# The state's part of a linear-attention output, computed per head in quarters of the array, with a compact state

## Chip, cores and metric

One core of a Trainium2 chip runs the whole kernel in one launch. The metric is the device time of an execution in microseconds; lower is better. All inputs and the output are fp32 in device memory.

## What is computed

For 4 batches, 8 heads, 768 steps and a head size of 48, a linear attention with a decaying state per head, and on its output (3072 tokens of 384 values) a layer with three input matrices, a maximum and an output matrix:

```python
for t in range(768):
    cur = einsum('bhd,bhe->bhde', u * k[t], v[t])
    y[t] = einsum('bhd,bhde->bhe', r[t], state + cur)
    state = w[t][..., None] * state + einsum('bhd,bhe->bhde', k[t], v[t])
x = y.transpose(0, 2, 1, 3).reshape(3072, 384)
h = maximum(maximum(x @ w1, x @ w2), x @ w3)      # 384 -> 768
out = h @ w_out                                   # 768 -> 384
```

## The kernel before

**Tiling.** The recurrence is done in chunks of 128 steps (`C`), 6 per batch and 24 in all, numbered k (`NK`). The 8 heads stand as 4 pairs (`NP`): the first head of a pair in partitions 0 to 47, the second in 64 to 111. The layer works on 512 tokens at a time, a "half" in the program's words, so there are six of them, each fed by 4 chunks (`CPH`). The first half's layer uses plain fp32 matmuls; the other five split every operand into a high and a low part and use three matmuls for one.

**The steps of a chunk** have one letter each (line 459). `b`, `f`, `r` (L309 to L335): running products of the decay by two scans on VectorE, then r and k are scaled by them; `b` also copies the chunk's total decay into `dec` on ScalarE, one copy for each head of the pairs (L315). `c` (L339) is a range check on ScalarE. `d`, `e` (L341 to L370): the diagonal term and the empty score tile. `X` scores (L374): per pair two matmuls of 48 partitions, one from partition 0 and one from 64, into two PSUM banks. `M` take (L386): VectorE copies the scores under the causal mask. `T` transposes (L395). `R` from_state (L404): what the state of all earlier chunks gives to the output, one matmul per pair, with the two heads' states as diagonal blocks of one 112 x 128 operand `sstar`, so the array sums over both heads' partitions and the zero blocks keep the heads apart. `U` to_state (L412): the chunk's contribution to the state, 8 matmuls into one bank; in chunks 1 to 3 it also adds the old state by two matmuls with the identity, one for each block column (L422). `S` state (L426): VectorE adds the old state (from chunk 4 on, one add for each head of the pairs, L433) and multiplies by the next chunk's decay, into both block columns at once (L435). `V` values (L439): scores times v, 8 matmuls that add to R's result in the tile `y`. `E` result (L447): ScalarE copies `y` to the layer's input `x`; after four chunks, six small DMAs put the fourth pair's rows where the layer wants them. `n` loads.

R and the first step of V write the same tile: `y` comes from a pool of one bank (`ps_y`), but chunks 1 and 3 take a bank of the layer's pool instead (`spare`, L406), and so do their scores (L377). PSUM's eight banks go: two for scores, one for `y`, one for T and U, four for the layer (`ps_m`, L187 to L190). The layer's pool also serves the small matmuls of `e` in the first 8 chunks (L356) and warm-up matmuls (`W`, L472).

**Order.** All engines work in program order. The strings at L67 to L70 write the order of the steps out by hand: a letter, then how many chunks ahead; `|` ends a unit. FRONT is used for chunks 0 to 2, LAST for 3, TURN and ORD for 4, ORD for the rest. In FRONT, R of the next chunk is issued at the end of a chunk (`R1`), before that chunk's M and V; in ORD, R of a chunk stands first, followed by X of the next chunk, U and V. A second string (START, L73) mixes units (`a`), weight conversions (`c`, `f`) and layer groups (`m`); later one group of the layer follows another and units are put in evenly (L604).

**The layer** (`moe_groups`, L111). A group is one bank: 6 plain or 9 split matmuls of 512 columns (L144). Its reader is issued after the next group's matmuls: ScalarE's copy (L123) for the first of three matrices, VectorE's maximum (L126) for the others. The output stage (L164) has four tiles of 384 columns, copied out by ScalarE (L168).

A second program part (from L611) repeats everything in another way where the range check fails; it does not run here.

Of the kernel before, what the change touches and what calls it, by code (L numbers as in the profile page):

```python
# [42 lines left out]
NP = 4  # L43
# [23 lines left out]
FRONT = "w U0 b1 | d1 f1 r1 | w e1 c1 S0 W2 X1 T1 | R1 M0 | V0 E0 n3 |"  # L67
LAST = "w M0 | V0 E0 U0 W9 n3 | b1 d1 | f1 r1 w | e1 c1 S0 X1 T1 R1 |"
# [19 lines left out]
def kernel(ctx: ExitStack, tc, tin, nat, u_flat, u_pair, v_t, w_all, out, ytr):  # L88
# [84 lines left out]
    with ExitStack() as fast:  # L173
# [16 lines left out]
        ps_m = pool("ps_m", 4, space=PSUM)  # L190
# [42 lines left out]
        sstar = [cst.tile([128, NP, 2, 64], F32, name=f"sstar{i}") for i in range(2)]  # L233
        dec = [cst.tile([128, LINE], F32, name=f"dec{i}")[:, 0:2 * NP].rearrange("p (a b) -> p a b", a=NP) for i in range(2)]
        for t in dec:
            nc.gpsimd.memset(t[:, :, :], 0.0)
        for t in sstar:
            nc.gpsimd.memset(t[:, :, :, :], 0.0)
# [70 lines left out]
        def prep_scan_b(k):  # L309
            gf = g_p.tile([128, lines(2 * WC)], F32, name="gf")[:, 0:2 * WC].rearrange("p (a b) -> p a b", a=2)  # L310
            t = tbuf[k % NB]
            nc.vector.tensor_tensor_scan(out=gf[0:112, 0, ::-1], data0=t[0:112, 0:WC][:, ::-1],  # L312
                                         data1=d_bwd[0:112, ::-1], initial=0.0, op0=ALU.mult, op1=ALU.add)
            for hh, rows in enumerate((slice(0, 64), slice(64, 112))):
                nc.scalar.copy(out=dec[k % 2][rows, :, hh], in_=gf[rows, 0, 1:WC:WS])  # L315
            prep[k] = dict(gf=gf)
# [86 lines left out]

        def from_state(k):  # L404
            p = prep[k]
            spare = k < CPH and k % 2  # L406
            p["y"] = y = ps_m.tile([128, NP, C], F32, name="psm") if spare else ps_y.tile([128, NP, C], F32, name="y")
            for pr in range(NP if k % NCH > 0 else 0):
                nc.tensor.matmul(y[:, pr, :], lhsT=sstar[k % 2][0:112, pr, :, :].rearrange("p a b -> p (a b)"),  # L409
                                 rhs=p["rp"][0:112, pr, :], start=(pr == 0), stop=True, skip_group_check=True)  # L410

        def to_state(k):  # L412
            if goes_on(k):
                p = prep[k]
                p["pu"] = pu = ps_tu.tile([128, 512], F32, name="tu")
                for pr in range(NP):
                    for q, m in ((0, 64), (64, 48)):
                        h = 2 * pr + (q > 0)
                        nc.tensor.matmul(pu[q:q + m, pr * D:(pr + 1) * D],  # L419
                                         lhsT=p["kn"][:, pr, q:q + m], rhs=natt[k][0][:, h * D:(h + 1) * D],  # L420
                                         start=(pr == 0), stop=(pr == NP - 1), skip_group_check=True)
                for hh in range(2 if k % NCH > 0 and k < CPH else 0):  # L422
                    nc.tensor.matmul(pu[0:112, 0:NP * D], lhsT=ident[0:112, 0:112], rhs=sstar[k % 2][0:112, :, hh, 0:D],
                                     start=False, stop=True, skip_group_check=True)

        def state(k):  # L426

            if goes_on(k):
                new = prep[k]["pu"][0:112, 0:NP * D].rearrange("p (a b) -> p a b", a=NP)
                if k % NCH > 0 and k >= CPH:  # L430
                    cur = scur[0:112, :].rearrange("p (a b) -> p a b", a=NP)
                    for hh, rows in enumerate((slice(0, 64), slice(64, 112))):
                        nc.vector.tensor_tensor(out=cur[rows], in0=new[rows], in1=sstar[k % 2][rows, :, hh, 0:D], op=ALU.add)  # L433
                    new = cur
                nc.vector.tensor_tensor(out=sstar[(k + 1) % 2][0:112, :, :, 0:D],  # L435
                                        in0=new.unsqueeze(2).broadcast_to([112, NP, 2, D]),
                                        in1=dec[(k + 1) % 2][0:112, :, :].unsqueeze(3).broadcast_to([112, NP, 2, D]), op=ALU.mult)

        def values(k):  # L439
            p = prep[k]  # L440
            for pr in range(NP):
                for q, m in ((0, 64), (64, 48)):
                    h = 2 * pr + (q > 0)
                    nc.tensor.matmul(p["y"][q:q + m, pr, :], lhsT=natt[k][0][:, h * D:h * D + m], rhs=p["a"][:, h, :],  # L444
                                     start=(k % NCH == 0 and pr == 0), stop=True, skip_group_check=True)

        def result(k):  # L447
# [5 lines left out]
            nc.scalar.copy(out=x[0:112, :, slot * C:(slot + 1) * C], in_=prep[k]["y"][0:112, :, :])  # L453
# [24 lines left out]
        def attn():  # L478
            for step in "bdfeWrRXTcW":
# [132 lines left out]
    with tc.If(rv != 0), ExitStack() as slow:  # L612
# [9 lines left out]
        with tc.For_i(0, B) as b:  # L622
            for pr in range(NP):
# [16 lines left out]
                for j in range(KT):  # L640
                    with tc.For_i(0, 16) as i:
# [21 lines left out]
                        for hh in range(2):  # L663
                            if pr < KT:
                                dst = ytr[pr, ds(i + 64 * hh + 16 * j, 1), ds(b, 1), :]
                            else:
                                dst = ytr[j, ds(i + 64 * hh + 48, 1), ds(b, 1), :]
# [41 lines left out]

def _layout(r, k, v, w, u, moe_w1, moe_w2, moe_w3, moe_w_out):  # L710
# [19 lines left out]
    for j in range(KT):  # L730
        for half in range(2):
            row[j, 64 * half:64 * half + 48] = (2 * j + half) * D + np.arange(48)
            row[j, 64 * half + 48:64 * half + 64] = (6 + half) * D + 16 * j + np.arange(16)
# [27 lines left out]
```

## Time and profile before

| | us |
|---|---|
| median of 3 runs | 435.39 |
| lowest and highest | 434.93, 436.48 |
| span of the profiled execution (its only time on the page) | 434.7 |
| TensorE busy in it | 422.1 |
| VectorE busy | 288.5 |
| ScalarE busy | 155.8 |
| GpSimd busy | 63.3 |

The span goes from the first to the last instruction of the profiled execution. PE is the matrix engine TensorE, PEld its weight loads, DVE VectorE, ACT ScalarE, POOL GpSimd, SP SyncE, which issues most DMAs. A group of the profile is all instructions of one line, engine and shape. The chain is followed back from the last instruction, at each step to what released it. Matmuls are pipelined and a group's mean duration is longer than the distance between two of them, so rates are read from the chain or from starts, not from the means.

### The profile page before, as it was taken

The numbers are of one execution on the slowest core, as the hardware profiler recorded it, in microseconds if no ns is written. First come the engines' busy times: TensorE is split into PE (matmuls) and PEld (weight loads), VectorE is DVE, ScalarE is ACT, GpSimd is POOL, SyncE is SP. The second block draws the span as 40 slices with busy tenths as digits, with TensorE's granted clock in tenths as the row PEclk, the third lists the DMA queues.
The fourth block names the chain that finished last, engine by engine and source line by source line (L and its number), as shares of the span: only waits on it lengthen the run. The fifth ranks groups of instructions, "written<-read, shape, count | busy, mean of one in ns | idle before, by whom it ended". The sixth has DMA issues, their size and how long they took to land.

```text
span 434.7 us, 7072 instructions
## 1 busy us (share of the span) xinstructions
PE 422.1 (97%) x2767; PEld 337.7 (78%) x2767; DVE 288.5 (66%) x520; ACT 155.8 (36%) x342; POOL 63.3 (15%) x69
## 2 busy tenths in 40 slices
PE   7997999999999999999999999999999999999994
PEld 3784645546788888988889988889988889988893
DVE  5999999999769987837658638648548624223310
ACT  1447554554453444423213423222523221312211
POOL 3120110020333030312112112202112100000000
PEclk9999999999999999999999999999999999999998
DMA  8883944344181403280411270340370000200001
GB/s 215 247 265 88 368 113 164 90 146 111 38 242 51 118 10 110 49 280 1 120 54 65 55 250 26 120 114 5 89 240 2 0 2 1 90 3 2 0 22 60
DMA packets 17244, 43.76 MB, mean 101 GB/s; under 512 B 2432, under 2 KB 8704, under 8 KB 17200
## 3 DMA queue, kind: packets, MB, share of 16 engines
q1 hardware_dynamic: 16832, 42.61, 32.1%
q10 hardware_dynamic: 368, 0.59, 0.5%
q8 instruction: 24, 0.39, 0.4%
q14 instruction: 20, 0.16, 0.1%
HBM read 37.30 MB, written 4.72 MB: 97 GB/s over the span
## 4 chain that ended last, share of the span: by engine, by line
PE 94%; DVE 2%; ACT 1%; DMA 1%; issue 0%; POOL 0%; DVEq 0%; POOLq 0%; ACTq 0%
PE psm L144 54%; PE psm L164 17%; PE gram L383 6%; PE y L444 5%; PE y L409 4%; PE tu L419 2%; PE psm L475 2%; PE tu L400 2%; PE psm L358 1%; DMA x<-x 1%; ACT cv L287 0%; ACT cv L271 0%; DVE x_lo L104 0%; DVE a L390 0%; DVE gf L323 0%
## 5 line engine op out<-in xcount | busy, mean ns | idle before, releaser
L144 PE MATMUL psm<-x_hi,w 128*128 128x512 f32 x540 | 172.7, 394 | 0.0
L144 PEld LDWEIGHTS psm<-x_hi,w 128*128 128x128 f32 x540 | 101.4, 188 | 22.8 <-issue 1.9
L144 PE MATMUL psm<-x_lo,w 128*128 128x512 f32 x270 | 105.2, 390 | 0.0
L126 DVE TENSOR_TENSOR m<-psm,m 128x512 f32<-128x512 f32 x60 | 41.4, 689 | 65.7 <-PE psm L144 54.3
L164 PE MATMUL psm<-w,h_hi 128*128 128x384 f32 x288 | 78.1, 364 | 0.0
L365 POOL TENSOR_SCALAR_AFFINE_SELECT a<-cs 128x1024 f32<-128x1024 f32 x24 | 26.6, 1108 | 257.5 <-DVE cs L362 174.9
L144 PEld LDWEIGHTS psm<-x_lo,w 128*128 128x128 f32 x270 | 50.7, 188 | 9.8
L164 PEld LDWEIGHTS psm<-w,h_hi 128*128 128x128 f32 x288 | 51.9, 188 | 7.0 <-issue 1.0
L144 PE MATMUL psm<-x,w 128*128 128x512 f32 x108 | 48.2, 597 | 1.3 <-DMA x<-x 1.3
L453 ACT COPY x<-y 112x512 f32<-112x512 f32 x22 | 12.9, 586 | 83.8 <-PE y L444 83.8
L103 ACT CAST h_hi<-m 128x512 fp32r<-128x512 f32 x30 | 18.6, 621 | 60.6 <-DVE m L126 60.5
L164 PE MATMUL psm<-w,h_lo 128*128 128x384 f32 x120 | 40.3, 335 | 0.0
L339 ACT ACTIVATE gf<-gf 112x1034 f32<-112x1034 f32 x24 | 25.6, 1068 | 37.6 <-DVE tin L334 36.0
L144 PEld LDWEIGHTS psm<-x,w 128*128 128x128 f32 x108 | 19.9, 190 | 24.1 <-issue 23.1
L312 DVE TENSOR_TENSOR_SCAN gf<-tin,d_bwd 112x517 f32<-112x517 f32 x24 | 29.4, 1225 | 9.8 <-DMA tin<-in_tin_dram 9.8
L104 DVE TENSOR_TENSOR h_lo<-m,h_hi 128x512 fp32r<-128x512 f32 x30 | 22.5, 750 | 20.2 <-ACT h_hi L103 20.2
L390 DVE COPY_PREDICATED a<-mask,gram 128x512 f32<-128x512 int32 x44 | 30.1, 741 | 0.3
L323 DVE TENSOR_TENSOR_SCAN gf<-tin,d_fwd 112x517 f32<-112x517 f32 x24 | 29.6, 1234 | 0.8
L383 PE MATMUL gram<-tin 48*128 48x128 f32 x352 | 25.6, 284 | 0.0
L383 PEld LDWEIGHTS gram<-tin 48*128 48x128 f32 x352 | 21.4, 187 | 5.2 <-issue 3.4
L444 PE MATMUL y<-a,v 128*48 128x128 f32 (+1 forms) x352 | 25.0, 276 | 0.0
L123 ACT COPY m<-psm 128x512 f32<-128x512 f32 x30 | 17.4, 581 | 20.3 <-PE psm L144 15.9
(78 smaller groups left out, 471.4 us busy)
## 6 DMA issues: line engine op xcount, KB each, us to landing
tin<-in_tin_dram SPq DMA_DIRECT2D x23, 677.7 KB, 5.2
w<-in_w_all_dram SPq DMA_DIRECT2D x24, 384.0 KB, 6.5
kr<-in_nat_dram SPq DMA_DIRECT2D x16, 384.0 KB, 5.5
v<-in_nat_dram SPq DMA_DIRECT2D x24, 192.0 KB, 4.7
out_dram<-m SPq DMA_DIRECT2D x24, 192.0 KB, 2.1
x<-x SPq DMA_DIRECT2D x33, 32.0 KB, 2.0
tin<-in_tin_dram SPq DMA_DIRECT2D x1, 258.0 KB, 4.8
tin<-in_tin_dram ACTq DMA_DIRECT2D x1, 193.5 KB, 3.5
```

Of the source, the lines that this page charges most:

```text
L103: nc.scalar.copy(out=hi, in_=src)
L104: rest = lambda: nc.vector.tensor_tensor(out=lo, in0=src, in1=hi.bitcast(F32), op=ALU.subtract)
L126: nc.vector.tensor_tensor(out=m[:, :], in0=ps[:, :], in1=m[:, :], op=ALU.max)
L144: nc.tensor.matmul(ps[:, :], lhsT=wt[f * 3 + wi][:, ct * 128:(ct + 1) * 128], rhs=xt[:, ct, :], start=(n == 0), stop=(n == KT * len(terms) ...
L164: nc.tensor.matmul(pss[tt][:, 0:DM], lhsT=ht[f][:, tok], rhs=wt[FT * 3 + f][:, :], start=(f == 0 and i == 0), stop=(f == FT - 1 and i == l ...
L312: nc.vector.tensor_tensor_scan(out=gf[0:112, 0, ::-1], data0=t[0:112, 0:WC][:, ::-1], data1=d_bwd[0:112, ::-1], initial=0.0, op0=ALU.mult, ...
L323: nc.vector.tensor_tensor_scan(out=gf[0:112, 1, :], data0=tbuf[k % NB][0:112, 0:WC], data1=d_fwd[0:112, :], initial=0.0, op0=ALU.mult, op1 ...
L339: nc.scalar.activation(out=flat, in_=flat, func=AF.Square, accum_out=acc[0:112, k:k + 1])
L365: nc.gpsimd.affine_select(out=a[:, :, :], in_=cs[:, :].unsqueeze(2).broadcast_to([128, H, C]), pattern=[[0, H], [1, C]], compare_op=ALU.is ...
L383: nc.tensor.matmul(gs[hh][:, pr, :], lhsT=p["kp"][q:q + 48, pr, :], rhs=p["rp"][q:q + 48, pr, :], start=(pr == 0), stop=(pr == NP - 1))
L390: nc.vector.copy_predicated(out=p["a"][:, hh::2, :], mask=mask_b(NP), data=p["gs"][hh][:, :, :])
L444: nc.tensor.matmul(p["y"][q:q + m, pr, :], lhsT=natt[k][0][:, h * D:h * D + m], rhs=p["a"][:, h, :], start=(k % NCH == 0 and pr == 0), sto ...
```

## The change

The state is kept compact: `sstar` has one block of 48 columns for a pair, padded with zeros to 64, instead of two block columns of 64, and `dec` one value for a pair and partition. R becomes 8 matmuls, one per head: head `hh` of pair `pr` is read from partitions 64*hh to 64*hh+47, and its result goes to columns of partitions 0 to 63 for pairs 0 and 1 and of partitions 64 to 111 for pairs 2 and 3. The tile `y` has two banks, one for the first head of every pair and one for the second. V's matmuls are ordered by the same places, and E reads 256 columns of each bank. The rows of the layer's input are thereby in another order, which the host's layout of the weights (`_layout`, L729) and the part that does not run follow. R is never issued from the layer's banks any more; that pool has three banks; and in FRONT R of the same chunk stands where R of the next one stood. In U, one identity matmul is left; in S, one add.

```diff
-FRONT = "w U0 b1 | d1 f1 r1 | w e1 c1 S0 W2 X1 T1 | R1 M0 | V0 E0 n3 |"
-LAST = "w M0 | V0 E0 U0 W9 n3 | b1 d1 | f1 r1 w | e1 c1 S0 X1 T1 R1 |"
+FRONT = "w U0 b1 | d1 f1 r1 | w e1 c1 S0 W2 X1 T1 | R0 M0 | V0 E0 n3 |"
+LAST = "w R0 M0 | V0 E0 U0 W9 n3 | b1 d1 | f1 r1 w | e1 c1 S0 X1 T1 R1 |"
...
-        ps_m = pool("ps_m", 4, space=PSUM)
+        ps_m = pool("ps_m", 3, space=PSUM)
...
-        sstar = [cst.tile([128, NP, 2, 64], F32, name=f"sstar{i}") for i in range(2)]
-        dec = [cst.tile([128, LINE], F32, name=f"dec{i}")[:, 0:2 * NP].rearrange("p (a b) -> p a b", a=NP) for i in range(2)]
-        for t in dec:
+        sstar = [cst.tile([128, NP, 64], F32, name=f"sstar{i}") for i in range(2)]
+        dec = [cst.tile([128, LINE], F32, name=f"dec{i}")[:, 0:NP] for i in range(2)]
+        for t in sstar:
             nc.gpsimd.memset(t[:, :, :], 0.0)
-        for t in sstar:
-            nc.gpsimd.memset(t[:, :, :, :], 0.0)
...
-            for hh, rows in enumerate((slice(0, 64), slice(64, 112))):
-                nc.scalar.copy(out=dec[k % 2][rows, :, hh], in_=gf[rows, 0, 1:WC:WS])
+            nc.scalar.copy(out=dec[k % 2][0:112, :], in_=gf[0:112, 0, 1:WC:WS])
...
+        def places():
+
+            return [(j, hh, half) for j in range(2) for half in range(2) for hh in range(2)]
+
         def from_state(k):
             p = prep[k]
-            spare = k < CPH and k % 2
-            p["y"] = y = ps_m.tile([128, NP, C], F32, name="psm") if spare else ps_y.tile([128, NP, C], F32, name="y")
-            for pr in range(NP if k % NCH > 0 else 0):
-                nc.tensor.matmul(y[:, pr, :], lhsT=sstar[k % 2][0:112, pr, :, :].rearrange("p a b -> p (a b)"),
-                                 rhs=p["rp"][0:112, pr, :], start=(pr == 0), stop=True, skip_group_check=True)
+            p["y"] = y = ps_y.tile([128, 2, NP, C], F32, name="y")
+            for j, hh, half in places() if k % NCH > 0 else ():
+                pr, m = 2 * half + j, 48 if half else 64
+                nc.tensor.matmul(y[64 * half:64 * half + m, hh, j, :], lhsT=sstar[k % 2][64 * hh:64 * hh + 48, pr, 0:m],
+                                 rhs=p["rp"][64 * hh:64 * hh + 48, pr, :], start=(j == 0), stop=True, skip_group_check=True)
...
-                for hh in range(2 if k % NCH > 0 and k < CPH else 0):
-                    nc.tensor.matmul(pu[0:112, 0:NP * D], lhsT=ident[0:112, 0:112], rhs=sstar[k % 2][0:112, :, hh, 0:D],
+                if k % NCH > 0 and k < CPH:
+                    nc.tensor.matmul(pu[0:112, 0:NP * D], lhsT=ident[0:112, 0:112], rhs=sstar[k % 2][0:112, :, 0:D],
                                      start=False, stop=True, skip_group_check=True)
...
-                    for hh, rows in enumerate((slice(0, 64), slice(64, 112))):
-                        nc.vector.tensor_tensor(out=cur[rows], in0=new[rows], in1=sstar[k % 2][rows, :, hh, 0:D], op=ALU.add)
+                    nc.vector.tensor_tensor(out=cur, in0=new, in1=sstar[k % 2][0:112, :, 0:D], op=ALU.add)
                     new = cur
-                nc.vector.tensor_tensor(out=sstar[(k + 1) % 2][0:112, :, :, 0:D],
-                                        in0=new.unsqueeze(2).broadcast_to([112, NP, 2, D]),
-                                        in1=dec[(k + 1) % 2][0:112, :, :].unsqueeze(3).broadcast_to([112, NP, 2, D]), op=ALU.mult)
+                nc.vector.tensor_tensor(out=sstar[(k + 1) % 2][0:112, :, 0:D], in0=new,
+                                        in1=dec[(k + 1) % 2][0:112, :].unsqueeze(2).broadcast_to([112, NP, D]), op=ALU.mult)
...
-            for pr in range(NP):
-                for q, m in ((0, 64), (64, 48)):
-                    h = 2 * pr + (q > 0)
-                    nc.tensor.matmul(p["y"][q:q + m, pr, :], lhsT=natt[k][0][:, h * D:h * D + m], rhs=p["a"][:, h, :],
-                                     start=(k % NCH == 0 and pr == 0), stop=True, skip_group_check=True)
+            for j in range(2):
+                for hh in range(2):
+                    for half, m in ((0, 64), (1, 48)):
+                        h = 4 * half + 2 * j + hh
+                        nc.tensor.matmul(p["y"][64 * half:64 * half + m, hh, j, :], lhsT=natt[k][0][:, h * D:h * D + m],
+                                         rhs=p["a"][:, h, :], start=(k % NCH == 0 and j == 0), stop=True, skip_group_check=True)
...
-            nc.scalar.copy(out=x[0:112, :, slot * C:(slot + 1) * C], in_=prep[k]["y"][0:112, :, :])
+            nc.scalar.copy(out=x[0:112, :, slot * C:(slot + 1) * C].rearrange("p (a b) n -> p a b n", a=2),
+                           in_=prep[k]["y"][0:112, :, 0:2, :])
...
-            for step in "bdfeWrRXTcW":
+            for step in "bdfeWrXTcW":
...
+def _head(place, half):
+
+    return 4 * half + 2 * (place % 2) + place // 2
...
-            row[j, 64 * half:64 * half + 48] = (2 * j + half) * D + np.arange(48)
-            row[j, 64 * half + 48:64 * half + 64] = (6 + half) * D + 16 * j + np.arange(16)
+            row[j, 64 * half:64 * half + 48] = _head(j, half) * D + np.arange(48)
+            row[j, 64 * half + 48:64 * half + 64] = _head(KT, half) * D + 16 * j + np.arange(16)
```

## Rows read from the trace of the kernel before

**Rows 1.** The page: span; busy us (share of span) xinstructions, by engine.
```profile
span 434.7 us, 7072 instructions
...
PE 422.1 (97%) x2767; PEld 337.7 (78%) x2767; DVE 288.5 (66%) x520; ACT 155.8 (36%) x342; POOL 63.3 (15%) x69
...
PE   7997999999999999999999999999999999999994
```

**Rows 2.** Windows A:B: length, busy us of each engine (x instructions), clock, DMA.
```profile
31.00:40.00 9.00, 6.76 (x72) 4.74 (x70) 9.00 (x22) 5.13 (x13) 0.19 (x1) 1.00 0.24 59
...
38.00:122.00 84.00, 82.71 (x427) 47.63 (x425) 77.28 (x158) 44.52 (x109) 10.72 (x9) 1.00 0.49 152
...
187.00:251.00 64.00, 64.00 (x464) 55.72 (x463) 41.24 (x67) 20.26 (x43) 12.37 (x12) 1.00 0.31 93
```

**Rows 3.** Chain in order of time, steady part: start us, us, what xrecords.
```profile
...
177.00 1.02 PE y L444 x15
...
224.40 0.89 PE y L409 x8
225.29 1.09 PE gram L383 x16
...
226.92 0.95 PE y L444 x16
```

**Rows 4.** Groups by form: line, engine, op, shapes xcount | busy us, mean ns | idle.
```profile
L383 PE MATMUL gram<-tin 48*128 48x128 f32 x352 | 25.6, 284 | 0.0
...
L409 PE MATMUL y<-tin,sstar 112*128 112x128 f32 x144 | 19.0, 274 | 0.0
...
L453 ACT COPY x<-y 112x512 f32<-112x512 f32 x22 | 12.9, 586 | 83.8 <-PE y L444 83.8
...
L315 ACT COPY dec<-gf 64x4 f32<-64x4 f32 x24 | 4.7, 194 | 0.7 <-DVE gf L312 0.7
...
L433 DVE TENSOR_TENSOR scur<-tu,sstar 48x192 f32<-48x192 f32 x13 | 4.7, 361 | 0.2
...
L433 DVE TENSOR_TENSOR scur<-tu,sstar 64x192 f32<-64x192 f32 x13 | 4.4, 340 | 3.3 <-PE tu L419 3.3
...
L435 DVE TENSOR_TENSOR sstar<-tu,dec 112x384 f32<-112x384 f32 x7 | 3.8, 546 | 0.0
...
L409 PE MATMUL psm<-tin,sstar 112*128 112x128 f32 x16 | 2.1, 276 | 0.0
```

**Rows 5.** Timeline of the start, by engine: start us, us, engine, line, what xcount [idle].
```profile
30.35 1.36 DVE L390 COPY_PREDICATED a<-mask,gram 128x512 f32<-128x512 int32 x2
...
33.06 1.35 DVE L390 COPY_PREDICATED a<-mask,psm 128x512 f32<-128x512 int32 x2
...
33.13 0.58 ACT L453 COPY x<-y 112x512 f32<-112x512 f32 x1 [1.41 <-PE y L444]
...
37.05 0.57 ACT L453 COPY x<-psm 112x512 f32<-112x512 f32 x1
...
27.29 0.90 PE L423 MATMUL tu<-sstar,ident 112*112 112x192 f32 x4
...
31.99 1.09 PE L444 MATMUL y<-a,v 128*64 128x128 f32 x16
...
39.96 6.25 PE L144 MATMUL psm<-x,w 128*128 128x512 f32 x14 [1.29 <-DMA x<-x]
```

**Rows 6.** Chain (first two), then timelines of TensorE, ScalarE and VectorE, 121 to 141 us.
```profile
127.20 10.43 PE psm L144 x45
...
138.02 4.10 PE psm L144 x18
...
121.19 0.69 PE L144 MATMUL psm<-x_hi,w 128*128 128x512 f32 x1
...
121.25 0.47 ACT L168 COPY m<-psm 128x384 f32<-128x384 f32 x1
...
139.85 0.68 DVE L126 TENSOR_TENSOR m<-psm,m 128x512 f32<-128x512 f32 x1
```

More of the change, by code (lines that the diff above doesn't have):

```diff
@@ L663 @@
                         for hh in range(2):
-                            if pr < KT:
-                                dst = ytr[pr, ds(i + 64 * hh + 16 * j, 1), ds(b, 1), :]
+                            place, lo = 2 * hh + pr % 2, 64 * (pr // 2)
+                            if place < KT:
+                                dst = ytr[place, ds(i + lo + 16 * j, 1), ds(b, 1), :]
                             else:
-                                dst = ytr[j, ds(i + 64 * hh + 48, 1), ds(b, 1), :]
+                                dst = ytr[j, ds(i + lo + 48, 1), ds(b, 1), :]
                             nc.sync.dma_start(out=dst.rearrange("a b t -> (a b) t"), in_=yo[hh:hh + 1, :])
```

## The prediction

> **What bounds the kernel now.** I read the page first. TensorE is busy for 97% of the span, VectorE for 66% [rows 1]. The stages say where that holds [rows 2]: from 31 to 40 us VectorE is busy throughout and TensorE for 6.8 of 9 us; from 38 us on TensorE is busy for practically the whole time (82.7 of 84 us, the gap being the wait for the first layer matmul), while VectorE falls from 77 of 84 us to 41 of 64. So after the start a microsecond saved on TensorE is a microsecond off the end, and one saved elsewhere is worth nothing unless TensorE would have waited for it.
>
> Next I read the chain in order of time, which gives each block of TensorE from the end of the one before to its own end. Of a chunk in the steady part it shows [rows 3] the state product R (L409) at 0.89 us, the scores X (L383) at 1.09 and, behind the state update U (L419), the values V (L444) at 0.95; where a batch ends there is no U, and V follows X. Every fp32 matmul leaves two records ("passes"), so R, four matmuls, has 8.
>
> **The rate of a pass.** R: 0.89/8 = 0.111 us a pass, with no gap to the layer's matmuls ahead of it, which use the whole array as R does. X has 16 passes, each as long as R's [rows 4]; one after the other they would take 16 x 0.111 = 1.78 us, and they take 1.09. X alternates between rows 0 to 47 and 64 to 111 of the array: two passes run side by side. V, 16 passes that alternate between two halves of the columns, takes 0.95: also two at a time. So 8 steps of 0.111 = 0.89 us stand in each, plus what it costs to change the division of the array: 1.09 - 0.89 = 0.20 us at X (behind R, whole array), 0.06 at V behind U (same division), and 0.13 where V follows X, at 1.02 us [rows 3].
>
> **The change, part by part.** *R in quadrants.* Per chunk 4 matmuls (8 passes) of 112 x 128 become 8 matmuls (16 passes) of 48 x 64 or 48 x 48, each in a quarter of the array, in an order that goes round the four quarters. No row shows four passes at once. Bounds: two at a time, as in X and V, 8 steps, 0.89 us; four at a time, 4 steps, 0.44 us. In X the two share all columns and differ in rows, in V they share all rows and differ in columns; both overlap fully, and nothing in either would forbid both divisions together. I take 4 steps. The block also changes the division behind the layer's matmuls, which R does not now: 0.06 to 0.20; I take the 0.20 of X, the nearest row (behind a whole-array block, rows divided). X behind it keeps its own 0.20. So R becomes 4 x 0.111 + 0.20 = 0.64 and a chunk gains 0.89 - 0.64 = 0.25 us. R has 144 + 16 records [rows 4], 20 chunks; 3 of them lie before 38 us, 17 after: 17 x 0.25 = **4.2 us**. With the switch at 0.06 it is 17 x 0.39 = 6.6; with steps in pairs the block takes 0.89 + 0.20 and the change costs 17 x 0.20 = 3.4.
>
> The Trainium skill's page "TensorE: Matmul & The Clock Gate", section "Part 3: Packing small matmuls — row/col tiling", says that a weight load overlaps matmuls in flight only when its row group differs. By that rule two quadrants on the same rows would not run together, the block would have 8 steps, and the sum would be the pair case, slower. V speaks against it: its two column halves use all rows, and their 16 passes still take 0.95 us, not 1.78 [rows 3].
>
> *State update.* In chunks 1 to 3 the second identity matmul goes (L423, four records in 0.90 us [rows 5], so some 0.4 us of TensorE each). In the start TensorE waits for VectorE anyway, so this is counted there, not apart. S on VectorE: the product that writes the state (L435) takes 0.55 us over 384 elements and will take about what L433 takes over 192, 0.35; from chunk 4 the two adds (0.34 + 0.36) become one of 0.36 [rows 4], 13 times. So 0.2 us per chunk in the start and 0.2 + 0.34 = 0.54 later. ScalarE loses one of two 0.19 us copies of the decay per chunk [rows 4]. After 38 us TensorE's full row covers all of these; if that cover were gone (VectorE the bound) they would be 13 x 0.54 = 7 us of gain, so they cannot hurt. Fewer zero fills on GpSimd let the first warm-up matmuls start earlier; the first useful matmul waits for VectorE's first product, so nothing comes of it, and without that cover it would be a gain.
>
> *The start.* VectorE is the full engine here [rows 2]; S of chunks 0, 1, 2 (L435) stands in its queue ahead of the masked copy M of chunk 2 at 30.35 [rows 5]. Three times 0.2 brings M forward by 0.6. V of chunk 2 starts at 31.99, right behind M and an R [rows 5]; that R drops from 0.89 to 0.64 and is chunk 2's now, not chunk 3's. Behind V, ScalarE's copy of the result starts at 33.13, then it works on to the result of chunk 3 at 37.05, and the first layer matmul, waiting for that result's transfer, starts at 39.96 [rows 5]. That chain moves forward by 0.6; bounds: 0 (if ScalarE meets something of its own) and 0.9 (M and the smaller R, 0.6 + 0.25, both in full). I take **0.6**.
> R of chunk k now waits for the result copy of chunk k-1, since there is one tile y. Behind the waiting R stand V, U and the small matmuls. For chunk 3, R comes directly behind that copy (33.13 + 0.58 = 33.7), and V behind it waits for its own M anyway, which is VectorE's 33.06 + 1.35 = 34.4 [rows 5]. V of 0.95 then ends near 35.4 and its copy does not start before 37.05, so over 1 us of cover is left; without it the first layer matmul would come later by the difference.
>
> *Three banks for the layer instead of four.* A layer tile may be taken up again once its reader is done; with three banks the third next group must wait. Where the readers run late: in the second half's layer a group ends at 135.5 (127.20 + 10.43 for five groups, less one of 2.1), VectorE reads it only from 139.85 to 140.53, and the group three later is the second of the two whose 18 matmuls follow 138.02, so from about 139.9 [rows 6]: 0.6 late. ScalarE reads the second output tile of the first half from 121.25 to 121.72; the next half starts at 121.19 [rows 6]: 0.5. Other places of this stage may add some tenths, 0.3 as an estimate; later VectorE has more room (41 of 64 us [rows 2]). So 0 to 1.4 us. VectorE is without a gap ahead of 139.85 and has one S there, which gets 0.54 shorter, and the second half's start waits for its own split input as well; I take **0.5 us lost**.
>
> *Order and result.* The copy of the result keeps 512 elements (0.586 us [rows 4]) but reads two banks: bounds 0 and 0.19, the price of a small ScalarE copy, felt only at the three tight hand-overs to the layer (start, 119, 370 us): 0 to 0.6; I take 0, it is one instruction of the same length. The new order of V's matmuls, of the output rows and of the host's layout moves no work; V still alternates between column halves. DMAs stay as they are in number and place; R, the one step that is moved, issues none.
>
> **Sum.** 4.2 + 0.6 - 0.5 = 4.3 us off the profiled 434.7. The runs shown have a median of 435.39, 0.7 above this span, so 435.4 - 4.3, rounded: **431.0 us**.
>
> **Rivals.** *Pairs only (slower).* The quarters run two at a time, as a mechanism: a weight load waits for the passes on its rows. Each later R takes 1.09 instead of 0.89, 3.4 us lost, banks 0.5 lost, of the start 0.3 kept: 435.4 + 3.6 = 439.0. It decides where a block has more than (0.89 - 0.20)/0.111 = 6 steps. For it: no row shows four at once. Against: both divisions, each by itself, overlap fully. It is what the rule of the Trainium skill's page "TensorE: Matmul & The Clock Gate", quoted above, would give. 0.11.
> *Something between.* Four passes at once stream four inputs and load four sets of weights; if a step takes 0.16 instead of 0.111, the chunk gains 0.05 and the whole 1 us: 434.5. 0.09.
> *A cheaper switch.* From layer to R 0.06, or X behind R for less than 0.20 since its rows are divided already: 6.6 + 0.9 - 0.5 = 7.0 gained, 428.4; both together, 17 x 0.14 more, would reach 426.0. 0.13.
> *Not in quarters at all.* If the matmuls were placed on the whole array, 16 passes one by one, 1.78: 17 x 0.89 = 15 us slower, 450. Against it, X's placing follows from where its operands lie, as it would here. 0.02.
>
> **How the numbers follow.** Forecast 0.65, the rest as above. 0.3%, 1.3 us, is about what a measurement of this kernel can tell from no change. Faster: forecast and cheaper switch, 0.78, and of "between" 0.03: 0.81. Same: the rest of "between", 0.06, and 0.02 of a forecast eaten up by banks (1.4) and hand-overs (0.6): 0.08. Slower: pairs less their best end, and no quarters, 0.11. The range goes from 427.4, the cheaper switch with most of its gain, to 434.4, the bank and hand-over bounds on top of a small gain per chunk; it leaves out pairs, no quarters, the best of the cheap switch and the worst of "between".
>
> **What would show it.** R's line with 320 records, in the chain at about 0.64 us a chunk where it stood at 0.89, X behind it still at 1.09; 0.9 or more in R would be the pair case. The first layer matmul at about 39.4. TensorE's idle time before layer matmuls, ended by VectorE or ScalarE near 121 and 140 us, is what the banks cost; over 1.5 us of it would prove that term wrong. The rest of the trace, the last half above all, should only be shifted.

## The result, and the profile after

The changed kernel takes 430.81 us (median of 4 runs, 429.29 to 433.03), the kernel before beside it 435.44 (434.93 to 436.48): ratio 0.988, 95% interval 0.984 to 0.993. Forecast were 431.0 us in a range of 427.4 to 434.4. The profiled execution took 429.43 us.

The page, to be read against [rows 1]: every engine has less to do, and TensorE is still busy for 97% of the span.

```profile
span 427.7 us, 7323 instructions
...
PE 413.4 (97%) x2921; PEld 323.6 (76%) x2921; DVE 278.7 (65%) x507; ACT 149.9 (35%) x318; POOL 63.1 (15%) x67
```

The chain in order of time (start us, us, what xrecords), against [rows 3], [rows 5] and [rows 6]:

```profile
37.99 7.96 PE psm L144 x18
...
118.94 2.06 PE psm L144 x9
...
134.99 4.10 PE psm L144 x18
...
220.19 0.59 PE y L410 x9
220.78 1.09 PE gram L380 x16
...
222.41 0.95 PE y L444 x16
```

R is now L410 and takes 0.59 us a chunk where it took 0.89; X (L380) behind it still takes 1.09 and V 0.95. The first layer matmul starts at 37.99 us instead of 39.96. From there to the end of the span it was 434.7 - 39.96 = 394.7 us and is 427.7 - 37.99 = 389.7. So the two profiled executions differ by 2.0 us in the start and by 5.0 in the rest, and the rest is about what R gives: the chain has 17 such blocks of R, and 17 x 0.30 = 5.1. Below, "the start" is the time to the first layer matmul and "the later part" what follows it.

Groups by form, to be read against [rows 4]:

```profile
L453 ACT COPY x<-y 112x512 f32<-112x512 f32 x24 | 14.1, 586 | 81.9 <-PE y L444 81.9
...
L410 PE MATMUL y<-tin,sstar 48*64 48x128 f32 x160 | 13.2, 282 | 0.7 <-ACT x L453 0.7
...
L410 PE MATMUL y<-tin,sstar 48*48 48x128 f32 x160 | 12.9, 279 | 0.0
...
L435 DVE TENSOR_TENSOR sstar<-scur,dec 112x192 f32<-112x192 f32 x13 | 4.6, 358 | 0.4
...
L433 DVE TENSOR_TENSOR scur<-tu,sstar 112x192 f32<-112x192 f32 x13 | 4.5, 348 | 3.1 <-PE tu L420 3.1
...
L435 DVE TENSOR_TENSOR sstar<-tu,dec 112x192 f32<-112x192 f32 x7 | 2.4, 345 | 0.0
```

R has its 320 records. S on VectorE is one add of 0.35 us and a product of 0.35. The result copy over two banks still takes 586 ns.

**The start** divides further. Timelines of TensorE and VectorE (start us, us, engine, line, what xcount [idle before and what ended it]), first of the kernel before:

```profile
8.89 3.46 PE L475 MATMUL psm<-warm 128*128 128x512 bf16 x8
...
22.77 0.59 PE L475 MATMUL psm<-warm 128*128 128x512 bf16 x2 [0.43 <-DVE cs L360]
...
6.35 0.69 DVE L345 TENSOR_TENSOR kr<-tin 112x512 f32<-112x512 f32 x1 [1.14 <-DMA tin<-in_tin_dram]
...
9.07 0.17 DVE L360 COPY cs<-psm 128x8 f32<-128x8 f32 x1 [0.47 <-PE psm L358]
...
16.29 0.17 DVE L360 COPY cs<-psm 128x8 f32<-128x8 f32 x1 [0.49 <-PE psm L358]
```

and of the changed kernel:

```profile
8.08 1.89 PE L476 MATMUL psm<-warm 128*128 128x512 bf16 x8
...
21.49 0.59 PE L476 MATMUL psm<-warm 128*128 128x512 bf16 x2 [1.57 <-DVE cs L357]
...
6.42 0.69 DVE L342 TENSOR_TENSOR kr<-tin 112x512 f32<-112x512 f32 x1 [1.09 <-DMA tin<-in_tin_dram]
...
15.22 0.16 DVE L357 COPY cs<-psm 128x8 f32<-128x8 f32 x1
15.30 0.35 DVE L435 TENSOR_TENSOR sstar<-tu,dec 112x192 f32<-112x192 f32 x1
```

Eight warm-up matmuls took 3.46 us before and 1.89 after, 0.43 and 0.24 us each, as at the lower and at the higher of TensorE's two clocks (1.2 and 2.4 GHz). The profile's clock column gives 1.00 for 8 to 12 us in both, so this first rise of the clock is read from the durations alone. VectorE waited 0.47 and 0.49 us for TensorE's small matmuls before, and did not wait there after. Those 1.0 us of the 2.0 are a difference between two executions, not between two kernels: below, variants of the changed kernel are seen with a late rise of the clock, and the kernel before, warmed up earlier, with an early one. What is the change's own is the longer wait ahead of the warm-up matmuls near 21.5 us, 1.57 us instead of 0.43: R, which stood in this place for the next chunk, now stands there for chunk 0, which has no state and no matmuls. The run with three banks alone, below, moves R in the same way and keeps the second identity matmul; there the wait is 1.47 us.

### The profile page after: what moved, and what is told of

It is laid out like the page before. It is cut to its first block, busy times and chain, and to the rows that moved or that the text cites. A ratio compares the mean times of both kernels' runs of the same rounds, so it can differ in the third digit from the quotient of the medians.

```text
span 427.7 us, 7323 instructions
## 1 busy us (share of the span) xinstructions
PE 413.4 (97%) x2921; PEld 323.6 (76%) x2921; DVE 278.7 (65%) x507; ACT 149.9 (35%) x318; POOL 63.1 (15%) x67
## 4 chain that ended last, share of the span: by engine, by line
PE 89%; DVE 6%; DMA 2%; ACT 1%; issue 0%; SPq 0%; DVEq 0%; ACTq 0%
PE psm L144 55%; PE psm L164 18%; PE gram L380 5%; PE y L444 5%; PE y L410 2%; PE tu L420 2%; PE tu L397 2%; DVE gf L320 1%; DMA tin<-in_tin_dram 1%; DVE gf L310 1%; PE psm L355 1%; DVE tin L331 1%; DVE a L387 1%; DVE kr L342 1%; DVE tin L330 1%; DMA x<-x 1%
## 5 line engine op out<-in xcount | busy, mean ns | idle before, releaser
L453 ACT COPY x<-y 112x512 f32<-112x512 f32 x24 | 14.1, 586 | 81.9 <-PE y L444 81.9
L444 PE MATMUL y<-a,v 128*48 128x128 f32 (+1 forms) x384 | 27.4, 276 | 0.1
L380 PE MATMUL gram<-tin 48*128 48x128 f32 x352 | 25.6, 284 | 0.9 <-DVE tin L331 0.9
L380 PEld LDWEIGHTS gram<-tin 48*128 48x128 f32 x352 | 21.4, 187 | 6.7 <-issue 4.3
```

The lines of the kernel that those rows point to most:

```text
L380: nc.tensor.matmul(gs[hh][:, pr, :], lhsT=p["kp"][q:q + 48, pr, :], rhs=p["rp"][q:q + 48, pr, :], start=(pr == 0), stop=(pr == NP - 1))
L444: nc.tensor.matmul(p["y"][64 * half:64 * half + m, hh, j, :], lhsT=natt[k][0][:, h * D:h * D + m], rhs=p["a"][:, h, :], start=(k % NCH == ...
```

## The experiments

Each ratio is against runs of the kernel before that were made beside it (medians of 435.17 to 435.47 us).

**The changed kernel once more**, beside the experiments below: 430.52 us (median of 6 runs, 429.41 to 436.18), ratio 0.988 (0.984 to 0.993).

> The changed kernel as it is, timed in five more rounds. Its four runs shown so far lie at 429.3, 429.4, 432.2 and 433.0 us. Theory: what differs between them is when TensorE's clock rises to 2.4 GHz in the start; then the spans differ by about 3 us while everything behind the first layer matmul has one length (389.7 us from there to the end), and runs come at about 429.4 and 432 to 433 again. Rival: the time is lost in the later part, at waits for the three banks; then the length behind the first layer matmul differs from run to run.

The time came out as before, but the runs scatter over 7 us, and this profile shows one reason. Windows (length, busy us of PE, PEld, DVE, ACT, POOL with counts, granted clock, DMA) of 23 to 27 us, first of the changed kernel's profile above, then of this one:

```profile
23.00:27.00 4.00, 4.00 (x67) 3.53 (x64) 3.93 (x7) 1.76 (x4) 0.00 (x0) 1.00 0.37 99
```

```profile
23.00:27.00 4.00, 4.00 (x53) 3.31 (x51) 3.93 (x7) 0.61 (x2) 0.00 (x0) 0.57 0.21 33
```

After the same wait (1.59 us here) TensorE was granted 0.57 of its full clock, that is 1.2 GHz for most of the stretch. The first layer matmul starts at 39.37 us instead of 37.99, and the later part is the same, 389.9. So the expectation was right on the later part and wrong on the cause: the eight warm-up matmuls near 8 us take 1.89 us in both profiles, and what differs is a fall of the clock behind the wait and not its first rise. It is not the whole scatter either. Each run lists its mean granted clock: 0.992 for this profile, 0.974 for the longest run (436.18 us), but 0.998 for the run of 434.89 us, which must have lost its time elsewhere.

**The order of the quarters.** Three kernels change only the order of R's eight matmuls, in `places()`. In the changed kernel neighbours are in all four quarters. Here, in turn, two quarters on different rows alternate first, then the other two; two on the same rows alternate; and both matmuls of a quarter stand together:

```diff
-            return [(j, hh, half) for j in range(2) for half in range(2) for hh in range(2)]
+            return [(j, hh, half) for half in range(2) for j in range(2) for hh in range(2)]  # row_pairs
+            return [(j, hh, half) for hh in range(2) for j in range(2) for half in range(2)]  # column_pairs
+            return [(j, hh, half) for half in range(2) for hh in range(2) for j in range(2)]  # in_turn
```

> The changed kernel with R's eight matmuls in another order: first the four for the columns 0 to 63, alternating between the two row halves, then the four for the other columns. If passes overlap only with neighbours in program order, R takes 8 steps: 0.44 us more than the 0.59 of the changed kernel, about 1.03 a chunk, and the kernel is 17 x 0.44 = 7.5 us slower than the changed one. If the engine sorts passes to free quarters over a distance of four matmuls, R keeps 0.59 and the time stays.

> The changed kernel with R's eight matmuls in another order: first the four on the rows 0 to 47, alternating between the two column halves, then the four on the rows 64 to 111. If neighbours overlap as well by columns as by rows, R takes 8 steps as with row pairs, about 1.03 us a chunk, 7.5 us in all more than the changed kernel. If passes on the same rows do not overlap, 16 steps: 1.78 + 0.15 = 1.93 us a chunk and 23 us more.

> The changed kernel with R's two matmuls of a quarter next to each other, one quarter after the other. If each quarter has its own order and the engine takes up passes for free quarters over a distance of eight matmuls, R stays near 0.60 us a chunk. If it looks only a few matmuls ahead, R needs more than 4 steps: 0.7 to 1.0 us.

R and X in their chains, row pairs, column pairs and in turn:

```profile
223.72 0.60 PE y L410 x16
224.32 1.09 PE gram L380 x16
```

```profile
223.16 0.61 PE y L410 x14
223.77 1.09 PE gram L380 x16
```

```profile
223.82 0.61 PE y L410 x14
224.43 1.09 PE gram L380 x16
```

R takes 0.60, 0.61 and 0.61 us, and the later parts are 389.9, 390.0 and 390.1: the order does not matter. All four quarters are at work together, also where the program gives them one after the other. With two matmuls of two passes each in a quarter in a row, an engine that starts passes strictly in order would need 3 + 3 + 3 + 4 = 13 steps of 0.111, or 1.4 us. So TensorE starts matmuls of free quarters ahead of earlier ones. The starts show it too. In turn, R's first record starts at 223.75 us, and the program's first eight records are all of the form 48*64. This is what has started in `y` by 223.85 us (count: ns min/median/max, first and last start us; forms):

```profile
L410 PE MATMUL y<-tin,sstar x4: 307/314/321, 223.8 to 223.8; 48*64 48x128 f32 x2, 48*48 48x128 f32 x2
```

Two records of 48*48, from the program's last four matmuls, run beside the first two of 48*64. That also answers the pair case of the prediction: the rule in the Trainium skill's page "TensorE: Matmul & The Clock Gate", section "Part 3: Packing small matmuls — row/col tiling", that a weight load overlaps only with matmuls of another row group, and the sentence behind it that matmuls start strictly in order, taken as the prediction took the first, do not hold here. With column pairs they would give 8 steps, at least 0.89 us; measured were 0.61.

The times are 432.41 us, ratio 0.990 (0.987 to 0.994); 433.13, 0.996 (0.992 to 1.000); and 432.36, 0.991 (0.988 to 0.994). They are above the changed kernel's 430.5, though not by the order of R: the profiled first layer matmuls start at 41.39, 40.79 and 41.51 us. In all three the clock fell in the start. With column pairs, where the eight warm-up matmuls took 1.89 us as in the changed kernel, this cost 40.79 - 37.99 = 2.8 us; with the two others these took 3.31 and 3.55 us besides. The window of 23 to 27 us with row pairs:

```profile
23.00:27.00 4.00, 4.00 (x37) 3.16 (x36) 3.93 (x8) 0.86 (x3) 0.37 (x1) 0.50 0.00 0
```

**Three banks alone.** The kernel before with three banks for the layer, R and the values always in `y`'s own bank, and the change's order of R; the state stays wide.

```diff
-FRONT = "w U0 b1 | d1 f1 r1 | w e1 c1 S0 W2 X1 T1 | R1 M0 | V0 E0 n3 |"
-LAST = "w M0 | V0 E0 U0 W9 n3 | b1 d1 | f1 r1 w | e1 c1 S0 X1 T1 R1 |"
+FRONT = "w U0 b1 | d1 f1 r1 | w e1 c1 S0 W2 X1 T1 | R0 M0 | V0 E0 n3 |"
+LAST = "w R0 M0 | V0 E0 U0 W9 n3 | b1 d1 | f1 r1 w | e1 c1 S0 X1 T1 R1 |"
...
-        ps_m = pool("ps_m", 4, space=PSUM)
+        ps_m = pool("ps_m", 3, space=PSUM)
...
-            p["y"] = y = ps_m.tile([128, NP, C], F32, name="psm") if spare else ps_y.tile([128, NP, C], F32, name="y")
+            p["y"] = y = ps_y.tile([128, NP, C], F32, name="y")
```

> The kernel before with three banks for the layer, y always in its own bank, and R of a chunk in the start at the place that it has in the changed kernel; R's matmuls, the state and S as before. My prediction's term: 0.5 us slower (0 to 1.4), with idle time of TensorE before layer matmuls near 121 and 140 us. Rival: the banks cost nothing in either kernel, ratio 1.000 within 0.1%.

Measured: 438.56 us (median of 12), ratio 1.005 (1.003 to 1.008). One of the twelve executions took 1484 us; there is no profile of it and its cause is open. The other eleven lie at 436.83 to 440.29 and give the ratio. The start is 40.59 us with a fallen clock, the later part 437.5 - 40.59 = 396.9, 2.2 longer than before. The waits of TensorE (who <- whom: us, times, longest), and the chain at the places:

```profile
PE psm L144 <- ACT m L168: 0.5, 1, 0.5
PE psm L144 <- DVE m L126: 0.3, 1, 0.3
```

```profile
73.69 0.70 DVE h_hi L126
...
74.43 7.99 PE psm L144 x18
...
122.62 0.38 ACT m L168
...
123.04 2.34 PE psm L144 x9
...
141.58 0.61 DVE m L126
...
142.24 2.37 PE psm L144 x9
```

The layer's matmuls now wait for the readers of the tile three groups back: VectorE's maximum near 74 and 142 us, ScalarE's copy of the output tile near 122. The last two are the places of [rows 6]. The waits listed are 0.8 us; what these places cost in all is seen from R behind the last two of them, in the chain of the kernel before and of this one:

```profile
123.73 0.89 PE y L409 x8
...
142.12 0.89 PE y L409 x8
```

```profile
125.39 0.89 PE y L408 x8
...
144.60 0.89 PE y L408 x8
```

Less the 0.63 us of the later start, this kernel is 1.0 us behind after the first and 1.9 after the second, of 2.2 at the end. In the changed kernel's chain, above, none of these waits stands: the groups at 118.94 and 134.99 follow other matmuls.

**S undone.** The changed kernel with the state's product on both block columns and the add in two parts again, as VectorE did it before; R and the identity matmul read the first block.

```diff
-        sstar = [cst.tile([128, NP, 64], F32, name=f"sstar{i}") for i in range(2)]
+        sstar = [cst.tile([128, NP, 2, 64], F32, name=f"sstar{i}") for i in range(2)]
...
-                    nc.vector.tensor_tensor(out=cur, in0=new, in1=sstar[k % 2][0:112, :, 0:D], op=ALU.add)
+                    for rows in (slice(0, 64), slice(64, 112)):
+                        nc.vector.tensor_tensor(out=cur[rows], in0=new[rows], in1=sstar[k % 2][rows, :, 0, 0:D], op=ALU.add)
...
-                nc.vector.tensor_tensor(out=sstar[(k + 1) % 2][0:112, :, 0:D], in0=new,
-                                        in1=dec[(k + 1) % 2][0:112, :].unsqueeze(2).broadcast_to([112, NP, D]), op=ALU.mult)
+                nc.vector.tensor_tensor(out=sstar[(k + 1) % 2][0:112, :, :, 0:D],
+                                        in0=new.unsqueeze(2).broadcast_to([112, NP, 2, D]),
+                                        in1=dec[(k + 1) % 2][0:112, :].unsqueeze(2).unsqueeze(3).broadcast_to([112, NP, 2, D]), op=ALU.mult)
```

> The changed kernel with S as it was: the product writes two block columns (384 elements) and the add is two instructions again; R in quarters, three banks and the short copy of the decay stay. From the first layer matmul to the end the kernel before took 394.7 us, three banks alone 396.9, the changed kernel 389.7. Theory: the 0.54 us that S saves on VectorE is what makes three banks free; then this length becomes 391 to 392, with waits of TensorE near the groups where three banks alone waited. Rival: the shorter R or the order makes them free and S is covered after the start, as my prediction said; then the length stays at 389.7 to 389.9. The start is 0.6 us later by either, apart from the clock.

Measured: 432.64 us, ratio 0.993 (0.991 to 0.996). The clock did not fall in this profile, and the later part is 429.2 - 38.28 = 390.9 us, 1.2 longer than in the changed kernel. Other runs agree: the three with a mean granted clock of 0.997 took 430.72 to 430.98 us, of the six of the changed kernel with 0.995 to 0.999 four took 429.29 to 429.50, one 430.06 and one 434.89. A wait of three banks alone is back, among TensorE's waits and in the chain:

```profile
PE psm L144 <- DVE m L126: 0.3, 1, 0.3
```

```profile
38.28 7.96 PE psm L144 x18
...
137.45 0.61 DVE m L126
...
138.11 2.33 PE psm L144 x9
```

Most of the 1.2 us is lost on the way to this group: R behind it starts at 140.44 us against 139.09 in the changed kernel, 1.06 more than the 0.29 of the start; at 124.73 us, against 124.17, it was still 0.27. So S's saving on VectorE is not hidden behind TensorE's full row. With three banks VectorE's reading sets at this place when TensorE may go on, and the shorter S is worth 1.2 us.

The run also gives S's share of the start. From VectorE's first product on the loaded chunk (6.10 us here, 6.42 in the changed kernel) the first layer matmul comes 32.18 us later here and 31.57 there: 0.6, as expected.

**A steady start.** The remaining runs are to show whether the wait near 21.5 us makes the clock fall. The first puts four warm-up matmuls (W4) in its place for chunks 1 and 2; the second also fills the warm-up operand ahead of all other GpSimd work and begins with 14 warm-up matmuls instead of 10, against the late first rise; the third is the second with W4 for chunk 1 alone; the last gives the kernel before the same early filling and the 14.

```diff
+FRONT2 = "w U0 b1 | d1 f1 r1 | w W4 e1 c1 S0 W2 X1 T1 | R0 M0 | V0 E0 n3 |"
...
+                for step in (FRONT if k < 1 else FRONT2 if k < CPH - 1 else LAST if k < CPH else TURN + ORD if k == CPH else ORD).split():  # first, second
+                for step in (FRONT2 if k == 1 else FRONT if k < CPH - 1 else LAST if k < CPH else TURN + ORD if k == CPH else ORD).split():  # third
...
-WARM = 10
+WARM = 14
...
+        warm = cst.tile([128, 128], BF16, name="warm")
+        nc.gpsimd.memset(warm[:, :], 0.0)
         ident = cst.tile([128, 128], F32, name="ident")
...
-        warm = cst.tile([128, 128], BF16, name="warm")
-        nc.gpsimd.memset(warm[:, :], 0.0)
```

> The changed kernel with four more warm-up matmuls for chunks 1 and 2 in the start, ahead of the small matmuls of the diagonal. Theory: in the slower runs TensorE's clock falls to 1.2 GHz at 21 to 23 us, behind 1.5 us in which it waits for VectorE; with this stretch filled the clock stays at 2.4 GHz from its first rise on, the first layer matmul starts near 38.0 in every run and the runs lie at 429.0 to 430.0 us, median 429.5. Rival: the fall has nothing to do with that wait; then runs of 430 to 433 us appear as often as without.

> The same four warm-up matmuls, and the first warm-up tile filled before everything else on GpSimd, with 14 instead of 10 warm-up matmuls at the start. Theory: TensorE starts near 1 us instead of 2.6, its clock rises before 7 us in every run, and the runs lie within 0.5 us of 429.3. Rival: the rise comes at a time of its own whatever the start is; then some runs keep a rise near 12 us and lie 1 us or more higher.

> The steady start with the four extra warm-up matmuls for chunk 1 alone, where TensorE's 1.5 us wait was; for chunk 2 they stood on the way, the scores began 0.9 us after VectorE had their input. Theory: the clock stays up, V of chunk 2 comes 0.5 us earlier, the first layer matmul at 37.7 instead of 38.25, runs near 429.3. Rival: without them the clock falls again in some runs, which then lie at 430.5 or more.

> The kernel before, with the first warm-up tile filled first and 14 warm-up matmuls, nothing else. If of the 2.0 us by which the first layer matmul came earlier in the changed kernel's first profile 1.0 belongs to an earlier rise of the clock and 1.0 to the change (S 0.6, R 0.4), this kernel's first layer matmul starts at 38.7 to 39.2 instead of 39.96 and its runs gain up to 1 us on the slower ones of before. If the rise is not what matters there, it stays at 39.9.

| | us, median | lowest to highest | ratio, 95% | profile: start / later part |
|---|---|---|---|---|
| W4 for chunks 1, 2 | 430.41 | 429.68 to 431.11 | 0.988 (0.986 to 0.990) | 39.51 / 389.9 |
| and early, 14 | 429.86 | 429.48 to 429.96 | 0.987 (0.985 to 0.989) | 38.25 / 389.9 |
| W4 for chunk 1, early, 14 | 429.37 | 429.06 to 430.59 | 0.986 (0.984 to 0.988) | 37.95 / 389.7 |
| before, early, 14 | 434.94 | 434.65 to 435.31 | 0.999 (0.997 to 1.000) | 38.47 / 394.5 |

The spread of the runs is down to 1.5 us or less. The third has the lowest median, though its interval and the second's overlap; its lines stand one to three lower than the changed kernel's. The first missed its expectation (429.5, start at 38.0) with a late first rise: its eight warm-up matmuls near 8 us took 3.42 us. The second and third kept the early rise in their profiles, as expected; the second's runs lie within 0.7 us of 429.3 and not 0.5, and the third's layer starts at 37.95 us and not 37.7. The kernel before started at 38.47 us, a little ahead of its 38.7 to 39.2.

On the fall of the clock the runs speak for the wait, but not for it alone. Their mean granted clock is a rough sign (three banks alone has 0.995 in its profile, fall included). In the changed kernel 4 of 10 runs have 0.992 or less, with the other orders 12 of 14, with S undone 7 of 10; with W4 none of 17, and in the kernel before with the early filling none of 12, is below 0.993. But 7 of the 59 runs of the kernel before made beside the experiments, at 437.9 to 438.6 us, have 0.988. So the clock seems to fall in some executions of that kernel too, whose wait at this place was 0.43 us in its profile; where in them it fell no trace shows. Timelines of TensorE and VectorE, of the third:

```profile
8.03 1.89 PE L477 MATMUL psm<-warm 128*128 128x512 bf16 x8
...
21.45 0.59 PE L477 MATMUL psm<-warm 128*128 128x512 bf16 x2 [0.40 <-DVE cs L360]
...
37.95 2.38 PE L145 MATMUL psm<-x,w 128*128 128x512 f32 x5 [1.43 <-DMA x<-x]
...
6.37 0.69 DVE L345 TENSOR_TENSOR kr<-tin 112x512 f32<-112x512 f32 x1 [1.24 <-DMA tin<-in_tin_dram]
...
28.63 1.35 DVE L390 COPY_PREDICATED a<-mask,gram 128x512 f32<-128x512 int32 x2
```

and of the last, the kernel before with a steady start:

```profile
7.87 1.89 PE L475 MATMUL psm<-warm 128*128 128x512 bf16 x8
...
38.47 1.95 PE L144 MATMUL psm<-x,w 128*128 128x512 f32 x4 [1.34 <-DMA x<-x]
...
5.96 0.69 DVE L347 TENSOR_TENSOR kr<-tin 112x512 f32<-112x512 f32 x1 [0.75 <-DMA tin<-in_tin_dram]
...
28.83 1.35 DVE L392 COPY_PREDICATED a<-mask,gram 128x512 f32<-128x512 int32 x2
```

Both run at 2.4 GHz here, so this pair gives the start at equal clock. From VectorE's first product on the loaded chunk (`kr`, whose load came 0.41 us later in one) to the masked copy M of chunk 2 it takes 28.83 - 5.96 = 22.87 us with the wide state and 28.63 - 6.37 = 22.26 with the compact one: 0.6, the three shorter S. To the first layer matmul it is 32.51 and 31.58: 0.9, the rest being put down to the smaller R. The third also has W4 for chunk 1, in a place where TensorE waited anyway (0.40 us are left of the wait).

## Why the prediction was right

**R in quarters** was right in kind and too small in size. The four steps hold: 0.59 us is less than the 0.89 of eight steps, whatever the order of the matmuls. The term that was mis-sized is the switch: "I take the 0.20 of X, the nearest row" should have been 0.59 - 4 x 0.111 = 0.15, between the bounds of 0.06 and 0.20. A chunk gains 0.30 and not 0.25, and 17 of them 5.1 us and not 4.2. The starts of R's records show that the steps are full ones and not longer: in the changed kernel they come in four sets of four, at 220.12, 220.28, 220.39 and 220.50 us, so the later sets are 0.11 us apart and the extra time lies outside them. The Trainium skill's page "TensorEngine Tiling (Array Packing)", section "Tiling Modes", says that changing the mode drains TensorE, which fits a fixed part in R and in X.

**State update and banks.** "After 38 us TensorE's full row covers all of these" is the step that failed, and it hid behind a net that came out well. The term for the banks, 0.5 lost out of 0 to 1.4, measured 0.1 in the changed kernel (5.1 from R against 5.0 in the later part). Yet three banks by themselves cost 2.2 us in the kernel before, over my upper bound, and undoing S in the changed kernel costs 1.2. So a saving that I put at nothing pays for a cost that I put too low. I had the two in one sentence ("one S there, which gets 0.54 shorter") and did not follow it: a busy row of TensorE says that it does not wait now, not that a shorter VectorE is worth nothing after a buffer is taken away. What removes the other 1.0 of the 2.2 was not tried by itself; one fewer copy of the decay on ScalarE, ahead of its wait near 122 us, is a candidate, and so is the shorter R.

**The start.** 0.6 was predicted with bounds of 0 and 0.9; at equal clock it is 0.9, the upper bound: M by 0.6, which S undone shows by itself, and 0.3 put down to the smaller R. ScalarE met nothing of its own: the result copies start at 31.04 and 35.05 us in the third version, against 31.61 and 35.55 in the kernel before with the steady start, although the chunk's load came 0.41 us later.

**R's move** I had only followed for chunk 3 and its wait for the result copy, and that cover held: R waits 0.7 us for that copy (L410 in the groups), and the first layer matmul still comes 0.9 earlier. What I left out is the place that R leaves: TensorE waits 1.57 us there, and afterwards the clock fell in some of the executions.

**Order, result, hand-overs** at nothing: right, 586 ns as before.

**The sum.** By the terms as measured, 5.0 + 0.9 = 5.9 us would have come off, against 4.3 forecast. The pair with a steady start shows 434.94 - 429.37 = 5.6. The change alone shows 435.44 - 430.81 = 4.6: without the steady start the median is 1.4 us higher after and 0.5 before, which the falls and late rises of the clock in some runs may explain. So two gains that were too small, a bank term that was too large and a missing one came out near the forecast; the mechanism of R was foreseen, the nearness of the sum was luck. (435.4 - 4.3 is 431.1, not 431.0.) My "0.7 above this span" was wrong also: 1.7 us lie outside the span (429.43 against 427.7). As 434.7 + 1.7 = 436.4, the profiled execution was near the slowest run shown, not near the median. The difference was taken from the median, so the error did not enter the time.

**Rivals.** Pairs only and not in quarters are refuted by R's 0.59 to 0.61 in four orders. "Something between" would have R at 0.84, and its longer steps do not show in the starts. The cheaper switch was half right, 0.15 for R's, while X's stayed at 0.20.

## What to carry to other kernels

Small fp32 matmuls whose operands and results can be laid on the four quarters of the array are worth placing there, in any order: here 16 passes took 0.6 us instead of 0.9 for 8 on the whole array. When a change takes a buffer away and shortens the reader of those buffers, price the two together, since the saving may be what pays for the loss. When a step is moved ahead of a wait, look also at the gap that it leaves in TensorE's row, and fill it if the kernel's start depends on the clock.

## What was not expected of the hardware

**Matmuls of free quarters start ahead of earlier ones** in the program: 0.61 us with both matmuls of a quarter together, where strict order would give 1.4. "All engines work in program order", in the section on the kernel before, is too strong for these small matmuls.

**The clock fell more often behind a wait in a stretch of small matmuls.** Seven profiles have a wait of 1.47 to 1.77 us ahead of the warm-up matmuls near 21.5 us; in five of them (the changed kernel once more, three banks alone and the three orders) TensorE was granted 1.2 GHz in most of the stretch that follows, in two (the changed kernel, S undone) it was not. In the five with a wait of 0.28 to 0.64 us (before, and the four steady ones) the clock stayed at 2.4 GHz. The fall costs 1.4 us in the second profile of the changed kernel and 2.8 with column pairs. Why it comes in one execution and not in another, and at times in the kernel before, was not found.

**The first rise of the clock comes early or late** from one execution to another, of the same program as well as of others. The eight warm-up matmuls near 8 us show it, at 1.89 us or at 3.3 to 3.6: late in the kernel before, row pairs, in turn and W4 for chunks 1 and 2; early in the changed kernel, both times, and in column pairs, three banks alone and S undone. The clock column gives 1.00 there in either case, so this is read from the durations. The variants of the changed kernel start their first warm-up matmul at 2.6 us with a late rise as with an early one, so a start at 2.6 us leaves it open. With the warm-up operand filled first and 14 matmuls all three profiles had it early. It is worth 1.0 us by VectorE's two waits in the kernel before.
